# Moving five maxima of the weight unpacking behind x of the second tile, and two unread products beside its transposes

## The chip, the cores and the metric

The kernel runs on one core of a Trainium2 chip. The metric is the device time of one execution in microseconds. A core has TensorE (PE in the profile, with PEld for its weight loads), VectorE (DVE), ScalarE (ACT), GpSimd (POOL) and SyncE (SP), whose queue starts the DMAs here. Each engine works through its own list of instructions in order; engines wait for each other on semaphores.

## The reference

Random-feature attention over 8 batches of 8 heads, 576 tokens and 64 dimensions, with 128 features, and then a feed-forward block on the 4608 x 512 result:

```python
def phi(x):                      # q and k, scaled by 1/sqrt(sqrt(D))
    proj = einsum('bhsd,md->bhsm', x, omega)
    h = proj - sum(x * x, -1, keepdims=True) / 2.0
    return exp(h - max(h, -1, keepdims=True)) / sqrt(m)
kv  = einsum('bhsm,bhsd->bhmd', phi(k), v);  z = sum(phi(k), axis=2)
x   = einsum('bhsm,bhmd->bhsd', phi(q), kv) / (einsum('bhsm,bhm->bhs', phi(q), z)[..., None] + 1e-6)
h   = x.reshape(4608, 512) @ w_in        # 512 -> 2048
out = (h * tanh(softplus(h))) @ w_out    # 2048 -> 512
```

All inputs are float32 except the two weight matrices, which reach the kernel as 64-bit words (the bytes of float64) and are turned into float32 on the chip.

## The kernel before

**Tiles and chunks.** The 4608 tokens are 36 tiles of 128; two tiles make a chunk of 256, so that there are 18 chunks. `k_task` makes the key side of a pair of heads of one batch (its names in the profile are pk, mxk, ek, pkv, kvf and kv), `q_task` the query side of one tile (pq, mxq, eq, then pn, rd and x). `ff_in` multiplies a chunk by `w_in` (ph), `ff_out` multiplies the result g by `w_out` (po).

**Two number forms.** Most products work on a pair of float16 parts, a high and a low one, of each operand, three products for each. Before the weights have been scaled and split, the work at the beginning goes in float32: the key sides of batches 0 and 1 (`KF`), the first five query tiles (`QF`), and the whole feed-forward of chunk 0. A float32 matmul appears in the trace as two records.

**Unpacking the weights.** `w_in` and `w_out` come in eight blocks each (`NB`). For one block `w_task` (L171) issues a DMA, a Prelu on ScalarE (L182) that rescales the high words, and on VectorE a shift of the low words (L183), a shift-and-or that joins the two (L187), and a maximum over the block (L190, `wmax`). Only `w_scale` (L198) reads these maxima: it reduces the eight to one (`am_w`, L203), takes the maximum over the partitions on GpSimd (L114, `allm_w`), and makes the scale `s_w`. `w_split` (L206) then turns each block into two float16 parts, with a cast on ScalarE (L72) and a difference on VectorE (L83). Blocks 0 to 7 of `w_in` lie in slots 1 to 8: in the lists below, w_107 is block 0, w_110 block 3, w_111 block 4, and w_114 block 7.

**The first two tiles.** `q_first` (L581) serves the float32 tiles. For tiles 0 and 1 it transposes the features on TensorE (pt), multiplies by kvf (pn), and then on VectorE, for each half of the heads, adds and scales the denominator (L603), takes its reciprocal (L607) and makes x (L609). Four transposes on TensorE bring x into px (L626), and ScalarE copies px to xT (L627). With xT of both tiles there, TensorE begins with ph of chunk 0.

**Spins.** `spin` (L94) is a product whose result nothing reads. Sixteen stand at the kernel's beginning, and two stand behind the exponentials of each of the first six tasks (L366).

**What sets the order.** The function bodies are generators that an agenda runs slot by slot; a scheduler in the language's tile layer then places each engine's instructions by priority and by when it believes their inputs to be ready. `issue_after` (L168, used by `behind`) adds an order on one engine without a semaphore: the instructions in the block come behind the named one on that engine. `anchors` holds such instructions: number 30 + t is the one that makes the last x of tile t (L619). In the kernel before, `AN` and `AO` hold only `None`, so no block of weights is tied to anything.

**GpSimd.** Two kinds of work stand on GpSimd: the maximum over the partitions (`allm_v` for a batch's values, `allm_w` for a weight matrix), and the low parts of queries, keys, x and values (sq, sk, xs, vb, L81). Between the two kinds stands a row ISA (MODIFY_POOL_CONFIG in the trace), which sets GpSimd up for the other kind.

Of the kernel before, what the change touches and what calls it, by code (L numbers as in the profile page):

```python
# [14 lines left out]
AF = mybir.ActivationFunctionType  # L15
# [15 lines left out]
def tile_kernel(  # L31
# [11 lines left out]
    P = 128  # L43
# [23 lines left out]
    act, dve, pool = nc.scalar, nc.vector, nc.gpsimd  # L67

    def cast(eng, out, in_, scale=1.0):

        if eng is act:
            act.activation(out, in_, AF.Copy, scale=scale)  # L72
        elif isinstance(scale, float) and scale == 1.0:
            eng.tensor_copy(out, in_)  # L74
        else:
            eng.tensor_scalar_mul(out, in_, scale)
# [17 lines left out]
    def spin(n, left, right):  # L94
        pi = ps_o.tile([P, 512], F32, tag="o", name=f"spin{nc.next_id()}")
        for _ in range(n):
            nc.tensor.matmul(out=pi[:, 0:right.shape[1]], lhsT=left, rhs=right, start=True, stop=True)
# [3 lines left out]
    ident = const.tile([P, P], F32, name="ident")  # L101
# [47 lines left out]
    def flat32(slot):  # L149
        return slot.rearrange("p a b -> p (a b)").bitcast(F32)  # L150

    def fetch_w(n, i, dma):
        src = w_src[n](i)


        at = ({0: 0, 1: 1, 2: 2, 3: 3}, {7: 0, 6: 1, 3: 0})[n].get(i)
        if at is not None:
            raw = wo_t[:, 2 * at:2 * at + 2].rearrange("p a b c -> p (a b c)").bitcast(I64)
        else:
            raw = sb.tile([P, BW], I64, tag="g", name=f"raw{i}", bufs=GB)  # L160
        dma.dma_start(out=raw.rearrange("p (a b) -> p a b", b=src.shape[2]), in_=src)
        return raw

    @contextmanager
    def behind(nth):
        with ExitStack() as st:
            for ins in anchors.get(nth, ()):
                st.enter_context(tc.issue_after(ins))  # L168
            yield

    def w_task(i, name):  # L171

        n = 0 if name == "wi" else 1
        raw = loaded.pop(f"w{n}_{i}", None) or fetch_w(n, i, w_dma)
        yield W_LOAD
        word = raw.bitcast(I32).rearrange("p (n two) -> p n two", two=2)
        low, high = word[:, :, 0], word[:, :, 1]
        dst = flat32(slots[w_at(n, i)])
        di = dst.bitcast(I32)
        with behind((AN, AO)[n][i]):  # L180
            m = high.bitcast(F32)
            act.activation(m, m, AF.Prelu, scale=2.0 ** -112, alpha=-(2.0 ** 32))  # L182
            dve.tensor_single_scalar(out=di, in_=low, scalar=29, op=ALU.logical_shift_right)  # L183
        yield W_GAP
        did("w", n, i)
        with behind((AN, AO)[n][i]):
            dve.scalar_tensor_tensor(  # L187
                out=di, in0=high, scalar=3, in1=di, op0=ALU.logical_shift_left, op1=ALU.bitwise_or
            )
            dve.tensor_reduce(  # L190
                out=wmax[n][:, i:i + 1], in_=dst, axis=AX.X, op=ALU.max, apply_absolute_value=True
            )

    def w_at(n, i):

        return i + 1 if n == 0 else NB + i
# [30 lines left out]
    def did(*key):  # L227
        done[key] = done.get(key, 0) + 1

    def must(n, *key):  # L230
        assert done.get(key, 0) >= n, key
# [24 lines left out]
    for i in range(2):  # L256
        t = const.tile([P, 2, 10, D1], F16, name=f"vb{i}")
# [35 lines left out]
    anchors = {}  # L293
# [162 lines left out]
    def spans(lo, n):  # L456

        res = []
        for b in range(lo // S, (lo + n - 1) // S + 1):
            res.append((b, max(lo, b * S) - lo, min(lo + n, (b + 1) * S) - lo))  # L460
        return res
# [3 lines left out]
    def q_task(nth, t):  # L465
# [6 lines left out]
        if t < QF:  # L472
            yield from q_first(nth, t, e, off)
            return
# [90 lines left out]
    def x_parts(nth, t, x):  # L565
        c, off = t * P // CH, t * P % CH
        if c >= SC0:
            yield from x_sums(nth, t, x)
            return
        xs = sb.tile([P, 2, H * D], F16, tag="xs", name=f"xs{t}", bufs=2)  # L570
        xf = x.rearrange("p h d -> p (h d)")
        cast(act if nth < 20 else by("x", nth), xs[:, 0], xf)
        rest(by("xlo", nth), xs[:, 1], xf, xs[:, 0])
        yield 1
        nc.sync.dma_start_transpose(
            out=xT[c].rearrange("p a k s -> p (a k) s")[:, :, off:off + P],
            in_=xs.rearrange("p a c -> p (a c)"),
        )
        did("x", c)

    def q_first(nth, t, e, off):  # L581

        qp = sb.tile([P, H, P], F32, tag="ap", name=f"qp{t}", bufs=2)
        for g in range(2):
            hs = slice(4 * g, 4 * g + 4)
            pt = ps_a.tile([P, 4, P], F32, tag="a", name=f"pt{t}_{g}")
            for i in range(4):
                nc.tensor.transpose(out=pt[:, i, :], in_=e[:, 4 * g + i, :], identity=ident)
            cast(act, qp[:, hs, :], pt)
        yield 1  # L590
        x = sb.tile([P, H, D], F32, tag="x", name=f"x{t}", bufs=2)
        rd = sb.tile([P, H, 1], F32, tag="rd", name=f"rd{t}")
        for g in range(2):
            hs = slice(4 * g, 4 * g + 4)
            pn = ps_a.tile([P, 4, D1], F32, tag="a", name=f"pn{t}_{g}", padded_shape=[P, 4, P])
            for i in range(4):
                for b, lo, hi in spans(t * P, P):
                    must(HP, "kvf", b)
                    nc.tensor.matmul(
                        out=pn[lo:hi, i, :], lhsT=qp[:, 4 * g + i, lo:hi], rhs=kvf[b][:, 4 * g + i, :],  # L600
                        start=True, stop=True,
                    )
            dve.tensor_scalar(  # L603
                out=rd[:, hs], in0=pn[:, :, D:D1], scalar1=EPS, scalar2=1.0 if t * P < CH else TOP / TX,
                op0=ALU.add, op1=ALU.mult,
            )
            dve.reciprocal(out=rd[:, hs], in_=rd[:, hs])  # L607
            if t * P < CH:
                xt = dve.tensor_tensor(  # L609
                    out=x[:, hs, :], in0=pn[:, :, 0:D], in1=rd[:, hs].broadcast_to([P, 4, D]),  # L610
                    op=ALU.mult,
                )
                continue
            for b, lo, hi in spans(t * P, P):
                xt = dve.scalar_tensor_tensor(
                    out=x[lo:hi, hs, :], in0=pn[lo:hi, :, 0:D], scalar=vstate[b][2][lo:hi],
                    in1=rd[lo:hi, hs].broadcast_to([hi - lo, 4, D]), op0=ALU.mult, op1=ALU.mult,
                )
        anchors[30 + t] = (xt.ins,)  # L619
        if t * P >= CH:  # L620
            yield from x_parts(nth, t, x)
            return
        yield 1
        px = ps_a.tile([P, KT, P], F32, tag="a", name=f"px{t}")
        for i in range(KT):
            nc.tensor.transpose(out=px[:, i, :], in_=x[:, 2 * i:2 * i + 2, :], identity=ident)  # L626
        cast(act, xT0()[:, :, off:off + P], px)  # L627
        did("x", 0)

    def xT0():
        return xT[0].rearrange("p a k s -> p (a k s)").bitcast(F32).rearrange("p (k s) -> p k s", k=KT)
# [264 lines left out]
    WI0, FF0, V0, V1 = 0, 17, 0, 16  # L899
    W_LOAD, W_GAP, PRIO = 1, 1, 400  # L900

    AN = (None,) * 8
    AO = (None,) * 8

    W_LO = ('dddddddd', 'dddddddd')
    W_HI = ('aaaaaaaa', 'aaaaaaaa')
# [58 lines left out]
    for t in range(NT):  # L965
        last = (t * P + P - 1) // S
# [30 lines left out]
    for what in PREL.split():  # L997
        i = int(what[1:] or 0)
# [12 lines left out]
    for i in range(NB):  # L1011
        start(w_task(i, "wi"), WIS[i])
    for i in reversed(range(1, NB)):
        start(w_task(i, "wo"), WOS[i])
# [9 lines left out]
    next(fi, None)  # L1024
    fi, fo = ff_in(1), ff_out0()
    start(w_task(0, "wo"))
    at(slot[0] + W_LOAD + W_GAP + 2, scale_w, 1)
    for j in range(8):
# [70 lines left out]
```

## Time and profile before

| what | value |
|---|---|
| median of three runs | 965.56 us |
| the three runs | 962.86, 965.56 and 983.64 us |
| the profiled execution | 962.69 us, its span 960.8 us |
| TensorE busy | 940.9 us, 98% of the span |
| VectorE busy | 624.9 us, 65% |
| ScalarE busy | 633.9 us, 66% |
| GpSimd busy | 222.7 us, 23% |
| mean granted TensorE clock | 0.992 |

Times inside the trace count from the start of the span; 1.89 us of the profiled execution's time lie outside it. In a row of the timeline the columns are the start, the busy time, the engine, the source line, the operation, output and input, their shapes, the number of records, and in brackets the idle time of the engine ahead of it with what ended that. In a row of the table by stretches they are the stretch, its length, the busy time of the five engines with their numbers of instructions, the granted TensorE clock as a share of full speed, the DMA engines' share, and GB/s. The work that the change touches lies in the first tenth of the span.

### The profile page before, as it was taken

The numbers are of one execution on the slowest core, as the hardware profiler recorded it, in microseconds if no ns is written. First come the engines' busy times: TensorE is split into PE (matmuls) and PEld (weight loads), VectorE is DVE, ScalarE is ACT, GpSimd is POOL, SyncE is SP. The second block draws the span as 40 slices with busy tenths as digits, with TensorE's granted clock in tenths as the row PEclk, the third lists the DMA queues.
The fourth block names the chain that finished last, engine by engine and source line by source line (L and its number), as shares of the span: only waits on it lengthen the run. The fifth ranks groups of instructions, "written<-read, shape, count | busy, mean of one in ns | idle before, by whom it ended". The sixth has DMA issues, their size and how long they took to land. (4 is left out here: it accounts for less than half of the span.)

```text
span 960.8 us, 20397 instructions
## 1 busy us (share of the span) xinstructions
PE 940.9 (98%) x8568; PEld 679.3 (71%) x8568; DVE 624.9 (65%) x1080; ACT 633.9 (66%) x818; POOL 222.7 (23%) x141
## 2 busy tenths in 40 slices
PE   9999988999999999999999999999989999999998
PEld 6788873677677777777777777777756777777663
DVE  5879797587766666656575655788889656643330
ACT  4758875686877877768667775778776866332231
POOL 0000052242432322322133333222231332200000
PEclk9979999999999999999999999999999999999999
DMA  9866314431741346313431253423552145634410
GB/s 287 271 208 208 109 48 94 102 58 61 140 92 37 107 77 119 69 59 75 101 68 53 69 118 66 93 89 68 136 124 73 37 100 115 172 117 131 133 57 33
DMA packets 147403, 100.25 MB, mean 104 GB/s; under 512 B 112112, under 2 KB 124528, under 8 KB 147312
## 3 DMA queue, kind: packets, MB, share of 16 engines
q1 hardware_dynamic: 147312, 98.95, 41.2%
q8 instruction: 67, 1.10, 0.5%
q14 instruction: 24, 0.20, 0.1%
HBM read 58.95 MB, written 13.63 MB: 76 GB/s over the span
## 5 line engine op out<-in xcount | busy, mean ns | idle before, releaser
L858 PE MATMUL po<-wo,g 128*128 128x512 f16 x1632 | 375.2, 380 | 0.0
L689 PE MATMUL ph<-xT,w 128*128 128x256 f16 (+1 forms) x2816 | 344.8, 279 | 0.7 <-ACT xT L72 0.7
L689 PEld LDWEIGHTS <-w 128*128 128x128 f16 x2688 | 261.0, 98 | 47.3 <-issue 0.7
L858 PEld LDWEIGHTS <-g 128*128 128x128 f16 x1632 | 155.1, 98 | 163.9 <-issue 2.2
L83 DVE SCALAR_TENSOR_TENSOR g<-h,us,g 128x1024 f16<-128x1024 f32 (+3 forms) x92 | 120.2, 1316 | 36.8 <-ACT g L72 36.2
L834 ACT ACTIVATE h<-ph,us 128x512 f32<-128x512 f32 (+3 forms) x152 | 83.3, 573 | 77.6 <-PE ph L689 76.8
L81 POOL TENSOR_TENSOR sq<-fq,sq 64x1024 f16<-64x1024 f32 x31 | 69.0, 2227 | 159.1 <-issue 65.2
L81 POOL TENSOR_TENSOR sk<-fk,sk 64x1152 f16<-64x1152 f32 x24 | 60.5, 2520 | 111.5 <-ACT sk L72 86.9
L81 POOL TENSOR_TENSOR xs<-x,xs 128x512 f16<-128x512 f32 (+1 forms) x35 | 44.2, 1264 | 151.9 <-issue 68.0
L72 ACT ACTIVATE g<-h,us 128x1024 f16<-128x1024 f32 (+3 forms) x80 | 72.6, 932 | 1.2
L834 ACT ACT_TABLE_LOAD x55 | 70.6, 1283 | 1.0
L364 ACT ACT_TABLE_LOAD x53 | 68.0, 1283 | 4.2 <-DVE ek L358 3.3
L349 DVE TENSOR_REDUCE mxq<-pq 128x4 f32<-128x512 f32 x72 | 46.8, 682 | 31.7 <-PE pq L340 31.6
L792 PEld LDWEIGHTS <-w 128*128 128x128 f16 x1008 | 58.4, 98 | 5.9
L81 DVE TENSOR_TENSOR qn<-eq,qn 128x1024 f16<-128x1024 f32 x31 | 38.9, 1254 | 36.2 <-ACT qn L72 36.2
L349 DVE TENSOR_REDUCE mxk<-pk 128x4 f32<-128x512 f32 (+1 forms) x96 | 50.1, 548 | 18.0 <-PE pk L340 18.0
L834 ACT ACTIVATE h<-h,us 128x1024 f32<-128x1024 f32 (+2 forms) x16 | 14.7, 933 | 61.9 <-DVE h L801 61.9
L72 ACT ACTIVATE o<-po,us 128x512 f32<-128x512 f32 (+1 forms) x38 | 25.8, 680 | 40.1 <-PE po L858 40.0
L81 DVE TENSOR_TENSOR kp<-ek,kp 128x1152 f16<-128x1152 f32 x24 | 36.4, 1515 | 24.0 <-ACT kp L72 24.0
L364 ACT ACTIVATE eq<-eq,lnt 128x1024 f32<-128x1024 f32 x31 | 35.6, 1148 | 21.2 <-DVE eq L358 21.0
L81 POOL TENSOR_TENSOR vb<-vf,vb 128x640 f16<-128x640 f32 x24 | 39.4, 1641 | 40.6 <-DVE vb L74 28.7
L801 DVE TENSOR_TENSOR h<-p_s,h 128x512 f32<-128x512 f32 x30 | 20.2, 689 | 43.2 <-PE p_s L792 43.2
(140 smaller groups left out, 1156.9 us busy)
## 6 DMA issues: line engine op xcount, KB each, us to landing
w<-ds SPq DMA_DIRECT2D x48, 256.0 KB, 3.4
vf<-in_vL_dram SPq DMA_DIRECT2D x32, 325.0 KB, 3.3
fq<-in_qT_dram SPq DMA_DIRECT2D x36, 256.0 KB, 3.6
out_dram<-o SPq DMA_DIRECT2D x36, 256.0 KB, 2.3
fk<-in_kT_dram SPq DMA_DIRECT2D x24, 256.0 KB, 3.6
raw<-in_w_out_dram SPq DMA_DIRECT2D x5, 1024.0 KB, 8.9
wo<-in_w_in_dram SPq DMA_DIRECT2D x4, 1024.0 KB, 13.2
raw<-in_w_in_dram SPq DMA_DIRECT2D x4, 1024.0 KB, 15.2
```

Source lines behind the costliest of these rows:

```text
L72: act.activation(out, in_, AF.Copy, scale=scale)
L81: eng.tensor_tensor(out=out, in0=in_, in1=hi, op=ALU.subtract)
L83: eng.scalar_tensor_tensor(out=out, in0=in_, scalar=scale, in1=hi, op0=ALU.mult, op1=ALU.subtract)
L349: sub = dve.tensor_reduce(out=mx[:, lo:hi], in_=pp[:, :m, :], axis=AX.X, op=ALU.max, negate=by_act)
L364: last = act.activation(e, e, AF.Exp, bias=lnt)
L689: nc.tensor.matmul(out=ph[:, i, :], lhsT=wi(a, k, f) if c else wi0(k, f), rhs=xT[c][:, y, k, :] if c else xT0()[:, k, :], start=n == 0, st ...
L792: nc.tensor.matmul(out=ph[:, i, :], lhsT=left(gr, op_l, i, a, k), rhs=x_region(c, r)[:, y, k0 + k, :], start=n == 0, stop=n == len(mm) - 1,)
L801: dve.tensor_tensor(out=out, in0=bank, in1=in0, op=ALU.add)
L834: act.activation(h[:, :, lo:hi], ph[:, :, lo:hi], AF.Mish, scale=us[:, 0:1])
L858: nc.tensor.matmul(out=po[i], lhsT=gT[c, gr][:, a, f % FG, i * P:(i + 1) * P], rhs=wo(y, f), start=f == 0 and (a, y) == parts[0], stop=f = ...
```

## The change

Four rows of numbers set what stands behind what on one engine. For `w_in`, the Prelu of block 7 on ScalarE stands behind the copy of tile 1's px (anchor 101, new), the shift and the joining of blocks 5 to 7 on VectorE stand behind the last x of tile 1 (anchor 31), and so do the maxima of blocks 3 to 7. After the transposes of tile 1 two products are added whose right side is a half of tile 1's x and whose result nothing reads.

```diff
@@ w_task
-        with behind((AN, AO)[n][i]):
+        with behind(AP[i] if n == 0 else None):
             m = high.bitcast(F32)
             act.activation(m, m, AF.Prelu, scale=2.0 ** -112, alpha=-(2.0 ** 32))
+        with behind((AN, AO)[n][i]):
             dve.tensor_single_scalar(out=di, in_=low, scalar=29, op=ALU.logical_shift_right)
...
+        with behind(AM[i] if n == 0 else None):
             dve.tensor_reduce(
                 out=wmax[n][:, i:i + 1], in_=dst, axis=AX.X, op=ALU.max, apply_absolute_value=True
             )
@@ q_first
-        cast(act, xT0()[:, :, off:off + P], px)
+        last = act.activation(xT0()[:, :, off:off + P], px, AF.Copy)
+        anchors[100 + t] = (last.ins,)
         did("x", 0)
+        if t == 1:
+            for hs in (slice(0, 4), slice(4, 8)):
+                spin(1, ident, x[:, hs, :].rearrange("p h d -> p (h d)"))
@@ tables
-    AN = (None,) * 8
+    AN = (None,) * 5 + (31,) * 3
+    AM = (None,) * 3 + (31,) * 5
+    AP = (None,) * 7 + (101,)
```

`cast` on ScalarE is the same activation as the one that now stands in its place. The lines of the changed kernel lie 1, 2, 6 or 8 higher than those of the kernel before from L183, L190, L631 and L902 on.

On VectorE, the rows around x of tiles 0 and 1 (x_441 and x_459) stand like this in the kernel before; the row behind the last is the second half of x_459:

```order
L190 TENSOR_REDUCE wmax_125<-w_110 128x1
L607 RECIPROCAL rd_442<-rd_442 128x4
L603 TENSOR_SCALAR rd_442<-pn_1_451 128x4
L609 TENSOR_TENSOR x_441<-pn_0_443,rd_442 128x256
L607 RECIPROCAL rd_442<-rd_442 128x4
L603 TENSOR_SCALAR rd_460<-pn_0_461 128x4
L609 TENSOR_TENSOR x_441<-pn_1_451,rd_442 128x256
L607 RECIPROCAL rd_460<-rd_460 128x4
L603 TENSOR_SCALAR rd_460<-pn_1_469 128x4
L609 TENSOR_TENSOR x_459<-pn_0_461,rd_460 128x256
L607 RECIPROCAL rd_460<-rd_460 128x4
L190 TENSOR_REDUCE wmax_125<-w_111 128x1
```

and like this in the changed kernel, where the first steps on pn_0_443 stand just ahead:

```order
L611 TENSOR_TENSOR x_441<-pn_0_443,rd_442 128x256
L605 TENSOR_SCALAR rd_442<-pn_1_451 128x4
L605 TENSOR_SCALAR rd_460<-pn_0_461 128x4
L609 RECIPROCAL rd_442<-rd_442 128x4
L609 RECIPROCAL rd_460<-rd_460 128x4
L605 TENSOR_SCALAR rd_460<-pn_1_469 128x4
L611 TENSOR_TENSOR x_441<-pn_1_451,rd_442 128x256
L611 TENSOR_TENSOR x_459<-pn_0_461,rd_460 128x256
L609 RECIPROCAL rd_460<-rd_460 128x4
L611 TENSOR_TENSOR x_459<-pn_1_469,rd_460 128x256
L192 TENSOR_REDUCE wmax_125<-w_110 128x1
L192 TENSOR_REDUCE wmax_125<-w_111 128x1
```

The two maxima have left the steps; the step that reads the last of the pn banks (pn_1_469) now stands ahead of the second half of x_441 and the first half of x_459.

On TensorE the same place, from the last pn on, stood like this before:

```order
L599 MATMUL pn_1_469<-kvf_160,qp_423 128x65 x4
L626 MATMUL px_481<-ident,x_441 128x128 x4
L626 MATMUL px_487<-ident,x_459 128x128 x4
L689 MATMUL ph_0_0_0_627<-xT_309,w_107 128x256
L340 MATMUL pq_0_514<-om_f,fq_498 128x128 x4
L340 MATMUL pq_4_519<-om_f,fq_498 128x128 x4
L340 MATMUL pq_0_526<-om_f,fq_500 128x128 x4
L340 MATMUL pq_4_531<-om_f,fq_500 128x128 x4
L689 MATMUL ph_0_0_0_627<-xT_309,w_107 128x256 x7
L588 MATMUL pt_0_557<-ident,eq_512 128x128 x4
L689 MATMUL ph_0_0_2_649<-xT_309,w_108 128x256 x3
```

and stands like this now:

```order
L628 MATMUL px_481<-ident,x_441 128x128 x4
L628 MATMUL px_487<-ident,x_459 128x128 x2
L97 MATMUL spin_494<-x_459,ident 128x256
L628 MATMUL px_487<-ident,x_459 128x128 x2
L97 MATMUL spin_497<-x_459,ident 128x256
L695 MATMUL ph_0_0_0_633<-xT_309,w_107 128x256 x5
L342 MATMUL pq_0_520<-om_f,fq_504 128x128 x4
L342 MATMUL pq_4_525<-om_f,fq_504 128x128 x4
L342 MATMUL pq_0_532<-om_f,fq_506 128x128 x4
L342 MATMUL pq_4_537<-om_f,fq_506 128x128 x4
L695 MATMUL ph_0_0_0_633<-xT_309,w_107 128x256 x3
L695 MATMUL ph_0_0_2_655<-xT_309,w_108 128x256 x5
```

A spin stands behind each pair of tile 1's transposes. Five products of ph stand ahead of pq of tiles 2 and 3 instead of one, and more of ph stands ahead of pt. Further on, too, the scheduler has put ph of chunk 0 earlier between the other products.

On GpSimd the rows from the maxima of `w_in` on were these, where fq_1054, fq_1267 and fq_1489 are the queries of tiles 5, 6 and 7, x_1113 is x of tile 4, and vam_1338 holds the values of batch 2:

```order
L114 ISA allm_w_638<-am_w_636 128x1
L114 ISA allm_v_748<-vam_746 128x1
L114 ISA allm_w_1103<-am_w_1101 128x1
L114 ISA allm_v_1340<-vam_1338 128x1
L81 ISA
L81 TENSOR_TENSOR sq_1171<-fq_1054,sq_1171 64x1024
L81 TENSOR_TENSOR xs_1141<-x_1113,xs_1141 128x512
L81 TENSOR_TENSOR sq_1307<-fq_1267,sq_1307 64x1024
L81 TENSOR_TENSOR vb_115<-vf_0_1254,vb_115 128x10x64
L81 TENSOR_TENSOR sq_1506<-fq_1489,sq_1506 64x1024
L81 TENSOR_TENSOR vb_120<-vf_1_1256,vb_120 128x10x64
```

and they are these now, with each number 6 higher:

```order
L114 ISA allm_v_754<-vam_752 128x1
L114 ISA allm_w_1109<-am_w_1107 128x1
L81 ISA
L81 TENSOR_TENSOR sq_1177<-fq_1060,sq_1177 64x1024
L81 TENSOR_TENSOR sq_1313<-fq_1273,sq_1313 64x1024
L81 TENSOR_TENSOR xs_1147<-x_1119,xs_1147 128x512
L114 ISA
L114 ISA allm_v_1346<-vam_1344 128x1
L81 ISA
L81 TENSOR_TENSOR sq_1512<-fq_1495,sq_1512 64x1024
L81 TENSOR_TENSOR vb_115<-vf_0_1260,vb_115 128x10x64
L81 TENSOR_TENSOR vb_120<-vf_1_1262,vb_120 128x10x64
```

The maximum of batch 2's values has moved behind sq of tiles 5 and 6 and xs of tile 4, and two more of the rows ISA stand around it. On VectorE the step that reads it (L132, p_v of batch 2) has moved in the same way: before, it stood ahead of x of tile 4; now it stands behind eq of tile 5 and ahead of the low parts of that tile's qn. From chunk 2's products and the keys of batch 2 on, the engines' lists are the same as before.

## The prediction

> **What bounds the kernel now.** I read the page's first part, then the table by stretches, then the timeline of TensorE where the table is not full.
>
> ```profile
> span 960.8 us, 20397 instructions
> PE 940.9 (98%) x8568; PEld 679.3 (71%) x8568; DVE 624.9 (65%) x1080; ACT 633.9 (66%) x818; POOL 222.7 (23%) x141
> 40.00:50.00 10.00, 8.06 (x58) 7.04 (x58) 9.13 (x20) 4.81 (x7) 0.00 (x0) 0.92 0.25 89
> 50.00:60.00 10.00, 10.00 (x37) 8.54 (x37) 8.69 (x16) 1.91 (x7) 0.35 (x1) 0.57 0.89 280
> 80.00:90.00 10.00, 10.00 (x62) 8.42 (x61) 10.00 (x15) 9.94 (x19) 0.00 (x0) 1.00 0.58 193
> 90.00:100.00 10.00, 10.00 (x67) 8.72 (x68) 10.00 (x13) 7.01 (x13) 0.00 (x0) 1.00 0.60 198
> 120.00:140.00 20.00, 17.30 (x177) 14.47 (x175) 19.39 (x42) 14.59 (x20) 8.93 (x6) 1.00 0.13 27
> 140.00:960.80 820.80, 807.89 (x7664) 569.38 (x7661) 514.76 (x883) 538.16 (x626) 211.45 (x119) 1.00 0.39 90
> ```
>
> TensorE bounds it: 98% busy, and 807.89 of the last 820.80 us. A microsecond won on TensorE at the beginning is therefore won at the end, unless another engine can't follow. The two weak stretches are 40 to 60, where the granted clock is 0.92 and 0.57, and 120 to 140, where VectorE is full. The first, closer:
>
> ```profile
> 48.00:48.50 0.50, 0.50 (x6) 0.50 (x6) 0.50 (x1) 0.00 (x0) 0.00 (x0) 0.83 0.00 0
> 48.50:58.50 10.00, 10.00 (x35) 8.71 (x35) 10.00 (x17) 1.14 (x4) 0.35 (x1) 0.50 0.74 220
> 58.50:59.00 0.50, 0.50 (x4) 0.39 (x3) 0.19 (x2) 0.00 (x0) 0.00 (x0) 0.93 1.00 401
> ```
>
> A mean of 0.83 means half clock for 0.17 us of that stretch, 0.93 for 0.07; with the 10.00 between, 10.24 us at half clock, which is 5.12 us of TensorE's work lost. What lies ahead, on TensorE and then on VectorE:
>
> ```profile
> 35.38 1.08 PE L97 MATMUL spin<-eq,ident 128*128 128x256 f32 x4
> 43.13 0.61 PE L626 MATMUL px<-ident,x 128*128 128x128 f32 x4
> 43.97 0.41 PE L626 MATMUL px<-ident,x 128*128 128x128 f32 x2 [0.23 <-DVE rd L607]
> 45.40 0.44 PE L626 MATMUL px<-ident,x 128*128 128x128 f32 x2 [1.02 <-DVE x L609]
> 46.52 0.70 PE L689 MATMUL ph<-xT,w 128*128 128x256 f32 x2 [0.69 <-ACT xT L72]
> 47.15 6.15 PE L340 MATMUL pq<-om_f,fq 64*128 64x128 f32 x32
> ...
> 43.33 0.16 DVE L603 TENSOR_SCALAR rd<-pn 128x4 f32<-128x4 f32 x1 [0.22 <-PE pn L599]
> 43.41 0.41 DVE L609 TENSOR_TENSOR x<-pn,rd 128x256 f32<-128x256 f32 x1
> 43.82 1.19 DVE L190 TENSOR_REDUCE wmax<-w 128x1 f32<-128x1024 f32 x1
> 44.93 0.41 DVE L609 TENSOR_TENSOR x<-pn,rd 128x256 f32<-128x256 f32 x1
> 45.26 1.28 DVE L183 TENSOR_SCALAR w<-raw 128x1024 int32<-128x1024 int32 x2
> ```
>
> TensorE waits 0.23, 1.02 and 0.69 us (1.94 together) between 43.1 and 46.5, and the longest of these is the maximum at 43.82. Between 43.13 and 46.52, 3.4 us, it does nothing but transposes; 1.8 us later the clock falls.
>
> **The change part by part.** *The maxima.* The last pn still ends at about 43.3, and the read of it now stands ahead of three steps of 0.41. They end near 44.6 and not 45.34; the transposes and the spins (0.54 each by the row at 35.38: two records of 0.27) then run to 46.0, and after ScalarE's copy ph begins at about 46.15 and not 46.52. Gain 0.4. Since VectorE now idles where the first maximum stood and does both after x, its shifts begin at about 44.6 + 2 x 1.15 = 46.9 and not 45.26: the scale of `w_in` comes some 1.6 us later.
>
> *The spins* add 1.08 us of TensorE's time, already inside the 46.15: one lies in the gap of 1.02, the other in the wait for the copy. If that cover were gone they would cost 1.08.
>
> *The clock.* From 44.55 on, TensorE's 3.4 us hold 1.1 of spins and 2.2 of ph, where there was idle time, transposes and pq. pq uses 64 rows of the array, and the trace shows it at full speed on its own:
>
> ```profile
> 7.93 3.50 PE L340 MATMUL pk<-om_f,fk 64*128 64x128 f32 x28
> 29.34 3.83 PE L340 MATMUL pq<-om_f,fq 64*128 64x128 f32 x32
> ```
>
> These took 0.12 us a record, at a granted clock of 1.00, and it did not fall behind them. I take the whole 5.12 us; the ends are 0 and 5.12. The Trainium skill speaks against this term: its page "TensorE: Matmul & The Clock Gate" (the table of goals under "Why this matters for your kernels") asks only that no idle gap exceed about 3 us, and by it gaps of 1.02 and 0.69 would not bring the clock down, nor would filling them keep it up; the sum would lack the 5.12. The same page (Part 4) says that transposes do not count as work for the clock, and with that the 3.4 us above are one such gap; the trace agrees so far as its fall follows them.
>
> *The stretch behind.* Here ScalarE bound TensorE already:
>
> ```profile
> 59.24 0.60 ACT L72 ACTIVATE g<-ph 128x512 f32<-128x512 f32 x1 [5.73 <-PE ph L689]
> 59.73 1.14 ACT L354 ACTIVATE eq<-pq,mxq 128x128 f32<-128x128 f32 x4
> 61.21 2.21 ACT L354 ACTIVATE eq<-pq,mxq 128x128 f32<-128x128 f32 x8
> 63.21 1.68 ACT L72 ACTIVATE qp<-pt 128x512 f32<-128x512 f32 x3
> ...
> 64.68 0.16 DVE L603 TENSOR_SCALAR rd<-pn 128x4 f32<-128x4 f32 x1 [6.00 <-PE pn L599]
> ...
> 67.16 4.54 PE L689 MATMUL ph<-xT,w 128*128 128x256 f32 x20
> ```
>
> At full clock ph's first bank is ready at about 53.7 and not 59.2, but tile 2's exponentials now wait for VectorE's later maxima: from 54 on, copy, four exponentials, a wait of some 1.1 for transposes, then 0.6, 1.1, 0.6, 2.2 and 1.7 lead to 62.6 and not 64.9. TensorE fills most of that with ph (0.23 a record), loses 0.6, ends pn at 65.0 and all of ph's third bank at 66.85. Before, that was 67.16 + 4.54 = 71.70. So TensorE is 4.9 us ahead there (0.4 + 5.1 - 0.6), VectorE only 64.68 - 62.3 = 2.4.
>
> *Do the others follow?* I walked the new lists with these durations to tile 4. ScalarE is tightest: it frees TensorE's banks some 1 to 1.5 us before they are needed, and tile 4's transposes wait about 0.4 for their exponentials. Equal work is then done some 4 us earlier: I take 0.9 off, with ends 0 and 2.5 (VectorE's own lead alone).
>
> *GpSimd.*
>
> ```profile
> 121.22 0.59 POOL L114 PARTITION_ALL_REDUCE allm_w<-am_w  x1 [43.07 <-DVE kv L76]
> 124.55 1.31 POOL L114 PARTITION_ALL_REDUCE allm_v<-vam  x1 [2.74 <-DVE vam L285]
> 132.74 2.23 POOL L81 TENSOR_TENSOR sq<-fq,sq 64x1024 f16<-64x1024 f32 x1 [6.88 <-ACT h L834]
> 135.05 2.02 POOL L81 TENSOR_TENSOR xs<-x,xs 128x512 f16<-128x512 f32 x1
> ...
> 231.02 0.38 POOL L114 PARTITION_ALL_REDUCE allm_v<-vam  x1 [6.13 <-DVE g L76]
> 238.43 2.13 POOL L81 TENSOR_TENSOR sq<-fq,sq 64x1024 f16<-64x1024 f32 x1 [7.03 <-issue]
> ...
> 135.03 1.07 PE L340 MATMUL pq<-om,sq 128*128 128x128 f16 x16 [2.70 <-POOL sq L81]
> 152.66 0.92 PE L495 MATMUL pn<-kv,qp 128*128 128x65 f16 x24 [3.03 <-DMA qp<-qn]
> ...
> 147.07 1.21 DVE L81 TENSOR_TENSOR qn<-eq,qn 128x1024 f16<-128x1024 f32 x1
> 148.31 1.87 SPq L481 DMA_TRANSPOSE qp<-qn  x1
> ```
>
> Each change between the kinds of work leaves GpSimd idle for 6 to 7 us (6.88, 6.13, 7.03). Now sq of tile 5 follows allm_w and this one change, not allm_v as well: allm_w at some 115 by the walk, sq done at 115 + 0.6 + 6.9 + 2.2 = 124.7, where TensorE comes to its pq at about 125.3. The wait of 2.70 goes; were allm_w only 4 us earlier than before, at 117.2, half of it would stay; the ends are 0 and 2.70.
>
> Against that, batch 2's allm_v comes only behind two sq, an xs and another change: 124.7 + 2.1 + 2.0 + 6.1 = 135. VectorE comes to `p_v` at about 131.5 and stands there until 135.5; queued behind are g, then qn's low part of tile 5; on ScalarE the scaling of vf waits with it. qn is done near 139, and by the rows at 148.31 and 152.66 pn follows 4.35 us after the transposes' issue, at 143.6. TensorE runs out at about 140.5 and waits 3.1: as long as before (3.03). vb and sq of tile 7 come some 7 us later on GpSimd, but their products stand behind all of chunk 0's po in TensorE's list. SP's queue gets qp of tile 5 ahead of a key load; qp of tile 6 still waits for its qn and not for the queue.
>
> **Sum.** 4.9 - 0.9 + 2.7 - 0.1 = 6.6 us. The profiled execution took 962.69 (1.89 outside the span): 956.1. Of the three runs shown, the lowest is 0.2 above it and the median 2.9; I add 0.9 and say 957.
>
> **Rivals.** *The clock falls all the same*, at the same place or at the 3.1 us wait by 140 (2.70 and 3.03 left it at 1.00). Price the same 5.1: 961 to 962. For it: the gaps filled are short and the decision is not in the trace; against: three spin places before, like the one at 35.38, kept 1.00. By the page's gap rule alone the fall would stay. 13%.
>
> *VectorE and ScalarE hold TensorE back.* VectorE is full from 80 to 100 (10.00 and 10.00) and has a lead of only 2.4; then that is all that arrives, and the GpSimd gain goes with it: 962.69 - 2.4 = 960.3, with the 0.9 961. 15%.
>
> *GpSimd's new trip lies on the path*, the slower side. allm_v, its two changes and what stands behind (6.1 + 0.4 + 7.0 = 13.5) stop VectorE at `p_v` and ScalarE at vf, the banks of ph aren't freed, and TensorE stands for all of it and not 3.1: 956.1 + 13.5 - 3.1 = 966.5, or 967. It decides from the point where allm_v ends 6.6 us after 135.4, at 142. For it: VectorE does wait there in my walk, and TensorE's 3.1 already hangs on it. 9%.
>
> **How the numbers follow.** The forecast has 60%, its own range 953 to 960; the rest, 3%, is something not seen. The low end takes the full gains and a third wait of 3.0 as well (4.9 + 2.7 + 3.0 = 10.6, so 952); the high end covers the two middle cases and most of the way to the slow one: 952.5 to 965.5. 2% (19 us) is about what this kernel's measurement tells from no change. No case reaches it: faster 2%; slower 3%, for a median like the run of 983.64; the same 95%.
>
> **What would show it.** Right: a clock of 1.00 from 46 to 60; ph at about 46.2 behind the last spin; ph's third bank done by 67; no wait at tile 5's pq; a VectorE wait of about 4 us at the `p_v` behind eq of tile 5; TensorE's wait ahead of pn of tile 5 near 3. Wrong: half clock anywhere from 46 to 60; waits of TensorE on ScalarE or VectorE between 67 and 125 of over 2 us together; a VectorE wait at that `p_v` of over 10.

## The result, and the profile after

The changed kernel takes 959.85 us (median of 20 runs, 957.01 to 980.78); the kernel before, run beside it, 965.5 us (20 runs, 959.05 to 983.64). The ratio is 0.9944, with a 95% interval of 0.9933 to 0.9955: 5.4 us faster, which by the bound of 2% is the same. The forecast was 957.0 in 952.5 to 965.5.

In some executions of every kernel here the clock already falls to half at 15 to 18 us and stays there for some 40 us; ratios and means below leave these out. The rows here come from an execution of the changed kernel of 961.58 us; where rows of another kernel's profile lie 17 to 19 us later, the text says so.

The first line of its page and three of its table by stretches (columns as before; the clock is the third figure from the right):

```profile
span 959.8 us, 20404 instructions
40.00:50.00 10.00, 9.38 (x66) 7.91 (x66) 8.04 (x18) 4.75 (x7) 0.00 (x0) 1.00 0.25 89
50.00:60.00 10.00, 10.00 (x61) 8.44 (x59) 10.00 (x17) 5.30 (x18) 0.35 (x1) 1.00 0.78 226
120.00:140.00 20.00, 17.46 (x137) 13.70 (x136) 19.47 (x43) 15.22 (x19) 6.08 (x4) 0.91 0.17 40
```

From 40 to 60 the clock is 1.00 where it was 0.92 and 0.57. But in 120 to 140 it is 0.91 now, where it was 1.00. The place of the change, on TensorE and then on VectorE:

```profile
43.78 0.83 PE L628 MATMUL px<-ident,x 128*128 128x128 f32 x4 [0.36 <-DVE x L611]
44.45 0.60 PE L97 MATMUL spin<-x,ident 128*128 128x256 f32 x2
45.10 0.60 PE L97 MATMUL spin<-x,ident 128*128 128x256 f32 x2
45.95 2.42 PE L695 MATMUL ph<-xT,w 128*128 128x256 f32 x10 [0.25 <-ACT xT L629]
48.31 3.83 PE L342 MATMUL pq<-om_f,fq 64*128 64x128 f32 x32
...
64.38 1.95 PE L695 MATMUL ph<-xT,w 128*128 128x256 f32 x8
```

```profile
44.18 0.42 DVE L611 TENSOR_TENSOR x<-pn,rd 128x256 f32<-128x256 f32 x1
44.52 2.33 DVE L192 TENSOR_REDUCE wmax<-w 128x1 f32<-128x1024 f32 x2
46.77 1.29 DVE L184 TENSOR_SCALAR w<-raw 128x1024 int32<-128x1024 int32 x2
```

TensorE is idle for 0.36 and 0.25 us where it was for 0.23, 1.02 and 0.69, and pq of tiles 2 and 3 takes 3.83 us in place of 6.15. The third bank of ph ends at 64.38 + 1.95 = 66.33 and not 71.70: TensorE is 5.37 us ahead.

Then the rows around tile 5's queries, on TensorE, ScalarE and GpSimd:

```profile
124.69 1.07 PE L342 MATMUL pq<-om,sq 128*128 128x128 f16 x16
135.25 4.45 PE L695 MATMUL ph<-xT,w 128*128 128x256 f16 x24 [2.53 <-ACT h L840]
143.83 0.91 PE L497 MATMUL pn<-kv,qp 128*128 128x65 f16 x24
160.13 0.92 PE L497 MATMUL pn<-kv,qp 128*128 128x65 f16 x24 [1.57 <-DMA qp<-qn]
189.96 0.62 PE L342 MATMUL pk<-om,sk 128*128 128x128 f16 x8 [0.30 <-DVE x L513]
```

```profile
124.85 0.67 ACT L840 ACTIVATE h<-ph,us 128x512 f32<-128x512 f32 x1
128.18 1.06 ACT L72 ACTIVATE sq<-fq 64x1024 f16<-64x1024 f32 x1 [2.65 <-DMA fq<-in_qT_dram]
132.05 1.15 ACT L366 ACTIVATE eq<-eq,lnt 128x1024 f32<-128x1024 f32 x1 [1.52 <-DVE eq L360]
134.51 0.69 ACT L840 ACTIVATE h<-ph,us 128x512 f32<-128x512 f32 x1
```

```profile
114.55 0.51 POOL L114 PARTITION_ALL_REDUCE allm_w<-am_w  x1 [49.90 <-DVE am_w L205]
122.51 4.22 POOL L81 TENSOR_TENSOR sq<-fq,sq 64x1024 f16<-64x1024 f32 x2 [7.45 <-issue]
134.36 0.38 POOL L114 PARTITION_ALL_REDUCE allm_v<-vam  x1 [6.07 <-DVE us L670]
```

The wait of 2.70 at tile 5's pq and the one of 3.03 ahead of its pn are gone. In their place TensorE stands 2.53 us ahead of chunk 1's ph, since ScalarE frees the bank only at 134.51 + 0.69 (its list now has tile 7's sq and tile 5's exponential, both waiting, ahead of that h), and 1.57 us at pn of tile 6. The waits of this place are 4.10 together, where they were 2.70 + 3.03 + 0.47 = 6.20. The two other profiles of the changed kernel have 2.22 and 2.23 at that ph, but also 1.46 and 0.96 at tile 5's pn, and 2.24 and 1.78 at tile 6's: 5.92 and 4.97 together, so that 4.10 is the least of three. In the execution shown here the first wait also brings the clock down:

```profile
132.61:136.02 3.41, 0.88 (x9) 0.68 (x8) 3.05 (x20) 3.38 (x4) 0.38 (x1) 1.00 0.00 0
136.02:139.43 3.41, 3.41 (x19) 2.43 (x17) 3.38 (x4) 3.17 (x5) 0.00 (x0) 0.50 0.00 0
```

3.41 us at half clock are 1.7 lost, so that this place brings 6.20 - 4.10 - 1.7 = 0.4. (Of the two others, one has such a spell behind tile 6's pn instead, the other none.) At the same pk (195.12 before, 189.96 now) the lead is 5.16.

Only 1.0 of it arrives at the end of this execution, because waits that both kernels have are longer in it. Before, and then after:

```profile
706.63 0.63 PE L340 MATMUL pk<-om,sk 128*128 128x128 f16 x8 [2.38 <-DVE x L511]
```

```profile
702.45 0.90 PE L342 MATMUL pk<-om,sk 128*128 128x128 f16 x8 [3.20 <-DVE x L513]
```

This wait, one at 242 (1.71 for 0.85) and one at 740 (2.30 for 1.50) are 0.8 to 0.9 us longer each, a fourth (0.62 at 719.11) is new, and behind 740 there is one more spell of 3.41 us at half clock: 3.1 + 1.7 us, less 0.4 at a wait that went (530.72). The wait at this pk is 3.25 and 3.27 in the other two profiles of the changed kernel as well, and 2.24 and 2.30 in those of its moves alone (below), so that it is not a matter of one execution; why it grows stays open. The ratio is that of the means, not of this execution.

**Clock and work apart.** Each execution has its mean granted clock, so its time can be split: span x (1 - clock) is lost to the clock, the rest is work and waits at full clock. Over 38 executions of the kernel before, the means are 964.5 us and 0.9904; over the 14 of the changed kernel from its first comparison, 959.15 and 0.9961. At full clock that is 964.5 - 9.2 = 955.3 and 959.15 - 3.7 = 955.5 (with clocks given to 0.001, good to about half a microsecond). On the means the whole gain is the clock: 9.2 - 3.7 = 5.5 us. All other terms come to nothing together.

### The profile page after: what moved, and what is told of

Same layout as the page of the kernel before. It is cut to its first block, busy times and chain, and to the rows that moved or that the text cites. A ratio compares the mean times of both kernels' runs of the same rounds, so it can differ in the third digit from the quotient of the medians.

```text
span 977.6 us, 20404 instructions
## 1 busy us (share of the span) xinstructions
PE 956.1 (98%) x8572; PEld 693.2 (71%) x8572; DVE 628.4 (64%) x1080; ACT 635.1 (65%) x818; POOL 223.6 (23%) x141
## 5 line engine op out<-in xcount | busy, mean ns | idle before, releaser
L351 DVE TENSOR_REDUCE mxq<-pq 128x4 f32<-128x512 f32 x72 | 46.9, 683 | 39.0 <-PE pq L342 39.0
```

What stands on the lines that cost most here:

```text
L351: sub = dve.tensor_reduce(out=mx[:, lo:hi], in_=pp[:, :m, :], axis=AX.X, op=ALU.max, negate=by_act)
```

## The experiments

All were timed beside the kernel before on the same chip, four kernels at a time. Which executions kept the clock at this place is judged by their mean clock, of which 10.24 us at half clock take 0.0053; falls elsewhere take their part too. TensorE's idle time is that between the first px and the first ph, from one profile of each kernel:

| kernel | idle, us | ratio, 95% | mean clock of the executions |
|---|---|---|---|
| before | 0.23 + 1.02 + 0.69 = 1.94 | 1 | 0.987 to 0.993 in 37 of 38, 0.998 in one |
| GpSimd's order alone | 1.94 | 0.9992, 0.9973 to 1.0011 | 0.990 and 0.991 (5) |
| px as ordinary products | 0.71 + 0.69 = 1.40 | 0.9982, 0.9952 to 1.0012 | 0.991 to 0.993 (3), 0.996 to 0.998 (3) |
| the two products alone | 0.23 + 0.58 + 0.26 = 1.07 | 0.9950, 0.9932 to 0.9968 | 0.994 to 0.999 (5) |
| transposes in their place | 0.23 + 0.58 + 0.25 = 1.06 | 0.9945, 0.9925 to 0.9964 | 0.994 to 0.996 (6) |
| the moves alone | 0.36 + 0.69 = 1.05 | 0.9940, 0.9923 to 0.9957; again 0.9925, 0.9902 to 0.9948 | 0.994 to 0.996 (8) |
| the moves and one product | 0.36 + 0.25 = 0.61 | 0.9919, 0.9903 to 0.9936 | 0.996 to 0.998 (4) |
| the whole change | 0.36 + 0.25 = 0.61 | 0.9944, 0.9933 to 0.9955; again 0.9964, 0.9943 to 0.9985 | 0.994 to 1.000 (19) |

**The whole change again, and its two halves.** First the unchanged new kernel:

> The changed kernel once more, for a profile in which TensorE's clock has not already fallen ahead of 40 us, as it had in the one profile of it. By the prediction: ratio to the kernel before 0.994; granted clock 1.00 from 46 to 60; ph at about 46.2; ph's third bank done by 67; no wait at tile 5's pq; a VectorE wait of about 4 us at batch 2's p_v; pn of tile 5 near 143.6 after a wait of about 3. By the rival that the clock falls all the same: half clock for 10 us between 46 and 60 and a ratio of 0.999.

The ratio was 0.9964 (0.9943 to 0.9985), which overlaps the first. In its profile the clock stays at 1.00 at this place, and tile 5's pq has no wait; but VectorE doesn't wait at batch 2's p_v, and TensorE waits 0.96 us at tile 5's pn and 2.23 at chunk 1's ph, not 3 at pn. Then the two products without the moves:

```diff
         did("x", 0)
+        if t == 1:
+            for hs in (slice(0, 4), slice(4, 8)):
+                spin(1, ident, x[:, hs, :].rearrange("p h d -> p (h d)"))
```

> The kernel before with the two unread products beside tile 1's transposes and nothing else: only TensorE's list differs, by these two. Theory A (the stretch of transposes and idle time brings the clock down, the unread products keep it up): clock 1.00 from 46 to 60, ph some 0.3 us later than before, then 4 to 5 us ahead where the clock was low, of which up to 1 is lost to ScalarE; GpSimd's 2.70 us wait stays. Gain 3 to 4.5 us, ratio 0.9955 to 0.997. Theory B (the single long gap that the maximum makes brings it down): the gap of 1.02 becomes 0.5 here, so half clock may go as well; if the clock falls, +0.3 us, ratio 1.000.

And the moves (the rows AN, AM and AP, and the two `behind`) without the products:

> The changed kernel without the two unread products: the moved maxima and what the scheduler makes of them alone. Theory A: no product but transposes for some 2.7 us still, and ph 0.7 us earlier than before; the clock falls as before, the gain of the moves is then 0.5 us and whatever the other order brings (0 to 2.7): ratio 0.997 to 1.000. Theory B (the maximum's gap): the clock stays at 1.00 and the ratio is 0.994 to 0.995.

The products alone gave 959.21 us in the median of all executions and a ratio of 0.995, the moves alone 958.65 and 0.994. TensorE at x with the products alone, and with the moves alone:

```profile
45.26 0.44 PE L626 MATMUL px<-ident,x 128*128 128x128 f32 x2 [0.58 <-DVE x L609]
45.53 0.60 PE L97 MATMUL spin<-x,ident 128*128 128x256 f32 x2
46.39 0.70 PE L692 MATMUL ph<-xT,w 128*128 128x256 f32 x2 [0.26 <-ACT xT L72]
47.02 3.83 PE L340 MATMUL pq<-om_f,fq 64*128 64x128 f32 x32
```

```profile
43.77 1.31 PE L628 MATMUL px<-ident,x 128*128 128x128 f32 x6 [0.36 <-DVE x L611]
45.77 2.86 PE L692 MATMUL ph<-xT,w 128*128 128x256 f32 x12 [0.69 <-ACT xT L629]
48.55 3.84 PE L342 MATMUL pq<-om_f,fq 64*128 64x128 f32 x32
```

Either half removes the fall (pq 3.83 and 3.84 for 6.15), and so the halves don't add. With the products alone the waits around tile 5 are those of before (2.73, 3.04 and 0.47) and the lead is 5.04 at pq of tile 5 and 5.02 at the pk of 195.12: nothing of it is lost in between. That the moves keep the clock without the products speaks against theory A, by which the stretch needs work that counts.

**Do transposes count for the clock?** First the eight transposes of px as ordinary products, with every list as before:

```diff
-            nc.tensor.transpose(out=px[:, i, :], in_=x[:, 2 * i:2 * i + 2, :], identity=ident)
+            nc.tensor.matmul(
+                out=px[:, i, :], lhsT=x[:, 2 * i:2 * i + 2, :].rearrange("p h d -> p (h d)"), rhs=ident,
+                start=True, stop=True,
+            )
```

> Before, with the eight transposes of px (tiles 0 and 1) issued as ordinary products against the identity; the lists of all other engines and the order on TensorE stay the same, so the waits on VectorE's x and on ScalarE's copy stay where they were (0.23, 1.02 and 0.69 us). Theory A, the clock falls because 3.4 us hold nothing but waits and transposes, which do not count for it: with counted products in that stretch the clock stays at 1.00 from 46 to 60, and the time falls by some 4 to 5 us as with either half of the change (ratio about 0.995). Theory B, the idle time itself (one gap of about 1 us, or 1.9 us in all) brings the clock down, whatever stands between: the clock falls at about 48 for 10.24 us again, and the ratio is 1.000, within 0.002.

Neither came true. The products take longer than the transposes, which shortens the idle time to 1.40 us:

```profile
42.93 1.56 PE L626 MATMUL px<-ident,x 128*128 128x128 f32 x12
45.20 0.71 PE L626 MATMUL px<-ident,x 128*128 128x128 f32 x4 [0.71 <-DVE x L609]
46.60 0.70 PE L692 MATMUL ph<-xT,w 128*128 128x256 f32 x2 [0.69 <-ACT xT L72]
```

Three executions kept the clock (958.44, 959.38 and 961.02 us), three did not (965.33, 965.44 and 965.61): 959.6 against 965.5, so that executions of one and the same kernel with and without the fall are 5.9 us apart, of which their mean clocks (0.997 and 0.992) explain 4.8. No single gap is longer than 0.71 us here, and yet half of the executions fell, while the moves alone have one of 0.69 and none of theirs did: the sum of the gaps fits, the longest one hardly does. Since idle time and the kind of work both changed, it doesn't part theory A from B. The next one does: the two unread products replaced by eight unread transposes, with the same idle time as the products alone.

```diff
-                spin(1, ident, x[:, hs, :].rearrange("p h d -> p (h d)"))
+                pi = ps_o.tile([P, KT, P], F32, tag="o", name=f"spin{nc.next_id()}")
+                for i in range(KT):
+                    nc.tensor.transpose(
+                        out=pi[:, i, :], in_=x[:, hs.start + i % 2 * 2:hs.start + i % 2 * 2 + 2, :], identity=ident
+                    )
```

> The two unread products of the run with the products alone (959.2, ratio 0.995, clock 1.00 from 46 to 60), each replaced by four unread transposes of the same half of x, 0.61 us for 0.54; every list but TensorE's stays the same. So TensorE is idle as short as there, some 1.0 us in place of 1.94, but the stretch from 43.1 to 46.5 holds nothing but transposes again, as in the kernel before. Theory A, transposes do not count for the clock: it falls at about 48 as before in most executions, and the ratio is 0.999 to 1.001. Theory B, only the idle time counts: the clock stays, and the ratio is 0.995, within 0.002.

The ratio was 0.9945, the clock 0.994 to 0.996 in all six. In its profile (shifted by 19 us) the stretch again holds nothing but transposes and waits, and pq behind it runs at full speed:

```profile
63.23 0.60 PE L633 MATMUL spin<-ident,x 128*128 128x128 f32 x4
64.41 0.44 PE L626 MATMUL px<-ident,x 128*128 128x128 f32 x2 [0.58 <-DVE x L609]
65.53 0.70 PE L696 MATMUL ph<-xT,w 128*128 128x256 f32 x2 [0.25 <-ACT xT L72]
66.17 3.83 PE L340 MATMUL pq<-om_f,fq 64*128 64x128 f32 x32
```

The clock is set in windows of 3.41 us (last section). The window over this place was busy for 2.58 us:

```profile
63.02:66.43 3.41, 2.58 (x16) 1.77 (x17) 3.41 (x5) 1.98 (x3) 0.00 (x0) 1.00 0.00 0
```

Of these, 1.68 us are transposes; without them 0.90 would be left, 26%. Every later window with so little was followed by half clock (last section), and this one was not. So transposes count for the clock, and with the idle time of the products alone they keep it as those do. Theory A falls; theory B, narrowed to the idle time of the whole stretch, agrees with every row of the table. That idle time is all that decides is not shown: two windows in the last section speak against it. The Trainium skill ("TensorE: Matmul & The Clock Gate", Part 4) says that the transpose mode "doesn't count as PE-busy the same way"; these runs show that it does count in this kernel.

**GpSimd's order.** Alone, with batch 2's allm_v behind sq of tile 6 and all else as before:

```diff
-        pool.partition_all_reduce(
-            out_ap=allm, in_ap=src, channels=P, reduce_op=bass.bass_isa.ReduceOp.max
-        )
+        with behind(("lo", "q6") if tag == "v2" else None):
+            pool.partition_all_reduce(
+                out_ap=allm, in_ap=src, channels=P, reduce_op=bass.bass_isa.ReduceOp.max
+            )
...
+        lo = rest(by("lo", nth), ks[D:P], f, ks[0:D])
+        anchors["lo", name] = (lo.ins,)
```

> The kernel before with batch 2's maximum over the partitions put behind sq of tile 6 on GpSimd, as the changed kernel has it, and nothing else; clock as before. By the prediction's term: sq of tile 5 is done near 131, TensorE's wait of 2.70 at its pq goes, the wait ahead of pn of tile 5 stays near 3: gain 1 to 2.7 us, ratio 0.997 to 0.999. By the rival of the slower side: VectorE and ScalarE stand at p_v and vf for the whole trip of 13.5 us, TensorE behind them: loss of up to 10 us, ratio 1.010.

And, on the other side, sq of tile 5 taken off GpSimd, on top of the two products:

```diff
-        rest(by("lo", nth), ks[D:P], f, ks[0:D])
+        rest(dve if name == "q5" else by("lo", nth), ks[D:P], f, ks[0:D])
```

> Before with the two unread products, and with the low part of tile 5's queries (sq) made on VectorE instead of GpSimd; the later low parts stay on GpSimd. My GpSimd theory, that the change between its two kinds of work (6.9 us) makes tile 5's pq late: the wait of 2.7 us at that pq goes. If that wait is then won on the path, TensorE stays ahead by it, and the time is 2 to 2.7 us below that of the two products alone (959.2): about 957, ratio 0.992. The rival, that what is won there is only waited for a few us later, because qn of tile 5 on VectorE and values on ScalarE are no earlier: the waits at tile 5's and 6's pn grow to 5 us together or more, and the time is that of the two products alone, ratio 0.995.

TensorE's pq and pn of tile 5 in the first (shifted by 17 us), then TensorE's and VectorE's rows in the second:

```profile
148.37 1.06 PE L342 MATMUL pq<-om,sq 128*128 128x128 f16 x16
167.59 1.50 PE L497 MATMUL pn<-kv,qp 128*128 128x65 f16 x24 [5.15 <-DMA qp<-qn]
```

```profile
125.94 1.06 PE L340 MATMUL pq<-om,sq 128*128 128x128 f16 x16
149.26 1.50 PE L495 MATMUL pn<-kv,qp 128*128 128x65 f16 x24 [8.39 <-DMA qp<-qn]
```

```profile
143.68 1.22 DVE L81 TENSOR_TENSOR qn<-eq,qn 128x1024 f16<-128x1024 f32 x1
```

In both the wait at tile 5's pq is gone, and in both it comes back at tile 5's pn: 5.15 in place of 2.70 + 3.03 + 0.47, ratio 0.9992 (a little above the 0.997 to 0.999 expected, which its interval doesn't exclude); and 8.39 + 0.49 in place of 6.24, ratio 0.9993 where the products alone had 0.995, worse than either expectation. Behind the 8.39 the clock also falls, for 6.83 us; the mean clock of this kernel's executions is 0.993, where the products alone had 0.996. In the second, tile 5's qn stands on VectorE behind maxima of values that a DMA brings (waits of 0.82 and 0.33 us), and begins only at 143.68, so that pn follows at 149.26, where the products alone had it at 147.63. That GpSimd's change of work (6.88 us before, 7.45 after) delays pq is true; that the end of this place hangs on it is not.

**Filling the wait at tile 5.** The moves alone have a fall of 6.8 us behind their wait at tile 5's pn. Eight unread products of tile 5's qn, and later three, were put ahead of that pn:

```diff
+        if t == QF:
+            pi = ps_a.tile([P, 512], F32, tag="a", name="spin_qn")
+            for _ in range(8):
+                nc.tensor.matmul(
+                    out=pi, lhsT=qn[:, 1, 0], rhs=qn[:, 1, 0:4].rearrange("p h m -> p (h m)"),
+                    start=True, stop=True,
+                )
```

> The moves of the maxima without the two products at x, but with eight unread products of tile 5's qn on TensorE where it waits for the transposes of that qn (2.4 and 1.0 us in the run of the moves alone). Theory A: with plain products in that wait the fall of 6.8 us at 141 goes, at 46 the clock stays at 1.00 as in the moves alone, and the time is some 3 us below the moves alone: about 955.5, ratio 0.991. Theory B, by which the fall follows single gaps of over about 1 us: the same for this place, as the gap is filled. If the products come at the wrong moment (they can only begin when qn is there, so most of the wait stands ahead of them), the fall stays and the time is that of the moves alone, 958.7, ratio 0.994.

> The moves alone with three unread products of tile 5's qn (0.22 us each) instead of eight, ahead of the last two products of chunk 0's po, so that they end inside the wait for the transposes. In the profile of the moves alone the stretch of 3.41 us that ends at 141.1, with TensorE busy 1.18 us of it (35%), is followed by 6.8 us at half clock; of the other such stretches with half-float products, those with 40% or less were followed by half clock and those with 41% or more were not. With 0.66 us more it would stand at 54%. Theory: no half clock at 138 to 148 in most executions, 2 to 3 us below the moves alone in this call: ratio 0.992 or less. Rival: the wait only splits otherwise over these stretches, which lie differently in each execution, or the products push what follows; then it is that of the moves alone.

With eight the ratio was 0.9963 (0.9942 to 0.9985), with three 0.9937 (0.9917 to 0.9957), where the moves alone in the call of the three had 0.9925. No gain. The three in the trace:

```profile
137.07 0.82 PE L484 MATMUL spin_qn<-qn 128*128 128x512 f16 x3 [1.64 <-DVE qn L81]
...
159.48 0.92 PE L504 MATMUL pn<-kv,qp 128*128 128x65 f16 x24 [2.81 <-DMA qp<-qn]
```

TensorE waits for qn itself (1.64 us), and then longer at tile 6's pn, where this execution's clock falls at 160.94: the rival of the second expectation.

**One product, and the moves again.**

> The moves with one unread product in place of two, behind the last transpose and ahead of ph. All lists but TensorE's are those of the moves alone, so that batch 2's maximum over the partitions stands behind sq of tile 5 alone, and not behind two sq and an xs as in the whole change. If the whole change is no better than its moves because of that order on GpSimd, this kernel goes as the moves alone (ratio 0.994 or a little less), with waits of some 4 us together at pq of tile 5, pn of tiles 5 and 6; if instead the product itself costs what it brings (0.54 us ahead of ph), it is 0.5 us slower than the moves alone.

> The moves alone once more, beside the two above. If the moves gain on GpSimd what the whole change does not, the ratio is again 0.994 or below, and the mean granted clock of its executions lies some 0.001 below that of the whole change (0.996) while its time is no longer. If the first reading was chance, the ratio is 0.995 to 0.996.

The moves and one product took 957.57 us in the median of all executions (0.9919, 0.9903 to 0.9936). The moves again had 0.9925, as expected if the first reading was not chance; their mean clock, 0.9957, hardly lies below the whole change's. Split by the clock as above, the moves alone come to 953.3 and 953.8 us at full clock, where the kernel before beside them comes to 954.9 and 955.9: a hint, from 5 and 3 executions, of some 2 us won besides the clock, which the whole change (955.5) doesn't have. With one product:

```profile
141.52 1.13 PE L497 MATMUL pn<-kv,qp 128*128 128x65 f16 x24 [2.70 <-DMA qp<-qn]
142.83 1.89 PE L342 MATMUL pq<-om,sq 128*128 128x128 f16 x16 [0.18 <-POOL sq L81]
...
159.88 0.92 PE L497 MATMUL pn<-kv,qp 128*128 128x65 f16 x24 [1.80 <-DMA qp<-qn]
...
189.66 0.62 PE L342 MATMUL pk<-om,sk 128*128 128x128 f16 x8 [0.25 <-DVE x L513]
...
701.02 0.62 PE L342 MATMUL pk<-om,sk 128*128 128x128 f16 x8 [2.33 <-DVE x L513]
```

This is the fastest kernel of the study, some 2 us below the whole change, though the two intervals just meet (to 0.9936, from 0.9933). Its waits around tile 5 are 4.68 together, no shorter than the 4.10 of the whole change, so that my reason, the order on GpSimd, isn't shown. The two profiles part later: at this pk they are 0.30 us apart (189.66 and 189.96), at the end of the span 4.4. In between this kernel waits 1.46, 2.33 and 1.50, 5.29 together, the whole change 1.71, 3.20, 0.62 and 2.30, 7.83 together, and the whole change has one more spell of half clock, 1.7. Why its late waits are longer isn't settled.

**A look for the profile.**

> The changed kernel once more, for its profile. Expected: clock 1.00 from 46 to 60, ph of chunk 0 some 0.45 us earlier behind its pn than before, no wait at tile 5's pq, waits of about 2 us at chunk 1's ph (on ScalarE) and 1.5 and 2 us at pn of tiles 5 and 6, as in the two profiles so far.

This is the execution shown above: all as expected up to 125 us; then 2.53 at chunk 1's ph (about 2 was expected), nothing at pn of tile 5 (1.5 was expected), 1.57 at that of tile 6 (2 was expected).

## Why the prediction was right, and where not

- *ph begins 0.4 earlier, at 46.15.* At 45.95, 0.57 earlier. The spins lie where the step put them. The second maximum now stands behind x, and the shifts begin at 46.77 (46.9 was said).
- *The clock, 5.12 us.* Right in size: 0.0057 of mean clock is 5.5 us, and in the kernel whose executions fall on both sides the mean clocks give 4.8. The reason named was half wrong: transposes do count, the moves alone keep the clock without the products, and the idle time of the stretch is what was too much, 1.94 us where 1.07 or less is not. That the term came out all the same is partly luck, since the change shortens the idle time besides adding products. The sentence by which the trace agreed with the Trainium skill on transposes went too far. The other rule of the Trainium skill ("TensorE: Matmul & The Clock Gate", "Why this matters for your kernels"), no idle gap over about 3 us, would have left the time as it was. The runs differ from it: the clock fell behind 1.94 us in three pieces, behind 2.38 (before, at 706.63) and behind 2.53.
- *ScalarE's stretch, -0.6, and -0.9 up to tile 4.* The third bank of ph ended 5.37 ahead (4.85 was said), so the first is -0.3. Between there and tile 5's pq TensorE waits once, 0.35 us for ek, in place of the 0.9; with the products alone the lead arrives whole. This term was too large: I let ScalarE's tight banks cost before the trace showed a wait.
- *GpSimd, +2.7 and -0.1.* This is the step that failed. allm_w ends at 115.1 (115 was said), sq of tile 5 near 124.6 (124.7), pq has no wait, allm_v ends at 134.7 (135), qn at 139.1 (139), pn begins at 143.8 (143.6): the chain over GpSimd and VectorE is as forecast. But VectorE reaches `p_v` only at 134.5 and waits 0.25 us there, not 4, and TensorE's wait of 3.1 isn't ahead of pn (0.96 and 1.46 stand there in the other two profiles). It stands earlier, 2.53 at ph, through ScalarE's list, which the step didn't walk in this place; and 1.57 us come at tile 6's pn. 2.1 us of waits go where 2.6 were forecast (0.3 and 1.2 in the other two), but the first wait costs 1.7 of clock: 0.4 remains in this execution. The two runs that free tile 5's pq by itself show next to nothing in the ratio either (0.9992, and 0.9993 where the products alone had 0.995).
- *The sum.* 6.6 was forecast at tile 6, 5.16 came there; the mean of the executions gains 5.4 (964.5 to 959.15). The 0.9 of the first waits was not needed and the 2.2 of GpSimd was not had. Nothing in the sum stands for the waits behind tile 6, which grew by 2.7 us in the profiles shown. The stated range reaches up to 965.5, the median of the kernel before itself, so that a time within it bears out none of the steps; the profiles do that.
- *The rivals.* From 46 to 60 the clock stayed. The first rival's other place, the wait by 140, did bring it down in the execution shown, for 1.7 us and not the 5.1 of its price; the other two profiles have no fall there. VectorE and ScalarE didn't hold the lead to 2.4. GpSimd's trip did not cost 13.5: allm_v was there by 134.7, far ahead of the 142 from which that rival would have decided.

## What to carry to other kernels

Where a trace shows half clock, add up the idle time of TensorE in the 3.4 us ahead of it: it pays to shorten any part of it. Either a moved step or an unread product did that here, and their gains don't add. A microsecond won at a wait of the bound engine is won only if the next engine in its list, here ScalarE with its waiting copies, is walked as well; a wait that is merely moved can bring the clock down where it lands; and part of a lead can be lost again in waits hundreds of microseconds later.

## What the runs showed of the hardware

**The clock is set on a grid of 3.41 us.** Every spell of half clock in 14 profiles is a multiple of it (3.41, 6.83, 10.24, up to 40.96 us), but for the last of each, which the end of the trace cuts off. Within a profile all of them begin on one grid, whose offset from the span's start differs: 0.54 us in the profile before, 1.17, 2.07, 2.58 and 2.89 in others. The Trainium skill ("TensorE: Matmul & The Clock Gate", Part 1) has a free-running window of 3413 ns; these traces agree.

**What a window needs.** Between 120 and 945 us, all 20 windows at full clock of the 14 profiles in which TensorE was busy for 40% or less were followed by half clock, and none with 44% or more; of eight with 41 to 43%, two were. The rows of 132.61 and 136.02 above are such a window (26% busy) and the one behind it. This fits that a wait of 3.03 us left the clock alone in the profile before: the grid cut it in two, and the longer part of it lay in a window that was 44% busy. In the float32 work at the beginning the busy share alone does not decide. The kernel before, and then the one with px as ordinary products:

```profile
44.91:48.32 3.41, 2.24 (x14) 1.67 (x15) 3.41 (x6) 1.06 (x2) 0.00 (x0) 1.00 0.00 1
48.32:51.73 3.41, 3.41 (x18) 3.41 (x18) 3.41 (x5) 0.00 (x0) 0.00 (x0) 0.50 0.16 22
```

```profile
43.03:46.44 3.41, 2.17 (x17) 1.78 (x16) 3.31 (x8) 2.13 (x3) 0.00 (x0) 1.00 0.02 8
```

The first window was busy for 2.24 of 3.41 us, 66%, and the clock fell; the last was busy for 2.17, 64%, and the clock stayed. The last holds little but products of px, which use all 128 rows. Half of the first is pq, which uses 64 of the array's rows and may count for less; that is argued, not shown, and no run here parts it.
